# Attention and two gated layers on one core: the short key chunk's products on all 128 rows, and one arrangement of transposed queries with a crossed copy

## The chip, the cores and the metric

The kernel runs on one core of a Trainium2 chip. The metric is the time of one execution on the device in microseconds (us), here the median of three runs. The engines of a core are TensorE (matrix products), VectorE, ScalarE, GpSimd and SyncE, which in this kernel issues the DMA transfers; a profile calls them PE (and PEld for TensorE's weight loads), DVE, ACT, POOL and SP.

## What is computed

There are 4 batches of 8 heads; each head has 576 positions of 64 numbers. Every head is an attention with a learned bias on the scores; the result goes through two feed-forward layers.

```python
scores = scale * np.matmul(q, k.transpose(0, 1, 3, 2))          # 576 x 576 a head
x = (psi_rel / psi_i)[..., None]                                # log distances
bias = np.maximum(x @ w1 + b1, 0.0) @ w2
scores = scores + bias.transpose(2, 0, 1)[None, :, :, :]
scores = scores - np.max(scores, axis=-1, keepdims=True)
attn = np.exp(scores)
attn = attn / (np.sum(attn, axis=-1, keepdims=True) + 1e-09)
y = np.matmul(attn, v)                                          # to 2304 x 512
g = y @ w_gate                                                  # 512 -> 1536
y2 = (g / (1 + np.exp(-g))) * (y @ w_val) @ w_out               # 1536 -> 512
out = np.maximum(y2 @ w_in, 0.0) ** 2 @ w_out2                  # 512 -> 2048 -> 512
```

## The kernel before, in words

**Numbers.** All operands are float32. For the products most of them are split into two float16 parts, a high one (hi) and the residual (lo), and hi·hi, hi·lo and lo·hi are summed, so that one wanted product is two or three products on TensorE.

**Passes.** Attention runs over five query tiles. Four tiles `t` = 0 to 3 hold 128 queries of a head, so each is a pass over 4 × 8 = 32 heads. The fifth, `"m"`, holds the last 64 queries: two heads stand side by side, so it has 16 items. `attend` (L936) takes the items one after the other: `scores` (L801), `soft` (L820, which adds the bias and exponentiates), `soft2` (L842, which transposes the probabilities) and, two items later, `weighted` (L864, the products with the values) and `normalise`. Beside each pass the bias of the next (`make_bias`), the weights and the first feed-forward layer (`moe1`, L459 and L482 its products) are computed; the second layer is worked out behind the attention, from about 770 us on.

**Key chunks.** A head's 576 keys are four chunks of 128 (keys 4·p + r for r = 0 to 3) and a short one of 64. In pass 0 the probabilities stay float32 and are transposed on TensorE; chunk 4 of the transposed probabilities holds the last 128 keys, and only its rows 64 to 127 are multiplied with the values' short chunk (L867). In the other passes a DMA transpose writes `pT` in nine chunks; chunk 4 holds the short chunk's hi part in rows 0 to 63 and its lo part in rows 64 to 127. Per head there are 14 products of 64 or 65 columns; the last, short chunk's hi with the values' lo part, takes rows 0 to 63 alone (`n = 64`, L876). Rows 64 to 127 of that part of the values are zeroed by a memset when they are made (L773). `kv_chunks`, `prep_k` and `turn` (L701, L713, L706) split the keys and transpose them on TensorE, the short chunk as 64 rows.

**Queries.** `prep_q` (L734) prepares four heads' queries of one tile: it loads `qf`, and writes into `qs` per head four blocks of 64 columns: hi, lo, lo, hi (ScalarE L746 both hi, VectorE L747 the residual, VectorE L754 its copy). A transpose makes `qT` of eight blocks of 128 × 128: per head one with hi over lo, and one crossed, lo over hi. `scores` multiplies both with the transposed keys (hi over lo) and sums them. In pass 0 the transposes are TensorE's (`turn`), in the other passes a DMA transpose's (L759). There are 36 such preparations: eight in pass 0, 28 in the other passes. `qs` and `qf` have one buffer each, `qT` has two. `attend` calls `prep_q` for the next four heads when it is at the first head of the present four (in the merged pass at the first item of a batch).

**Order.** The generators are interleaved by costs that stand in the `yield` lines and by a table (`LEAD`), which the change does not touch. The framework then orders each engine's instructions itself, by priorities and a simulated timeline, and puts in all waits on semaphores; on the chip every engine, SyncE among them, runs its list in order. All DMA transfers, the transposes included, are issued by SyncE.

Of the kernel before, what the change touches and what calls it, by code (L numbers as in the profile page):

```python
# [11 lines left out]
F16 = mybir.dt.float16  # L12
# [3 lines left out]
AF = mybir.ActivationFunctionType  # L16
# [8 lines left out]
P = 128  # L25
# [12 lines left out]
SQK = 16.0  # L38
# [37 lines left out]
def tile_attention_moe(  # L76
# [4 lines left out]
    nc = tc.nc  # L81
# [11 lines left out]
    ident_h = res.tile([P, P], F16, name="ident_h")  # L93
# [8 lines left out]
    st = {}  # L102
# [86 lines left out]
    def minus(out_, x, f, hi):  # L189

        nc.vector.scalar_tensor_tensor(
            out=out_, in0=x, scalar=f, in1=hi, op0=ALU.mult, op1=ALU.subtract)
# [21 lines left out]
    def mixed(k):  # L214

        mix_n[k] = mix_n.get(k, -1) + 1
        return MIX[k][mix_n[k] % len(MIX[k])]
# [176 lines left out]
    att = a_stack.enter_context(tc.tile_pool(name="att", bufs=2, side="right"))  # L394
# [5 lines left out]
    def ma():  # L400

        if early[0]:
            return ps_qk.tile([P, 2, 512], F32, tag="qk", name="qk0")[:, 0, :]
        return ps_mm.tile([P, 512], F32, tag="ma", name="ma", bufs=1)
# [248 lines left out]
    def load_kv(h, which):  # L653

        b, g = divmod(h, 2)
        hs = slice(4 * g, 4 * g + 4)
        src, f = ((k, kvroom(h)[0]), (v, kvroom(h)[3]))[which]
        nc.sync.dma_start(
            f[:, 0:1024].rearrange("p (h x) -> p h x", h=4),
            src[b, hs, 0:512, :].rearrange("h (p r) d -> p h (r d)", r=4))  # L660
        nc.sync.dma_start(
            f[64 * which:64 * which + 64, 1024:1280].rearrange("p (h d) -> p h d", h=4),
            src[b, hs, 512:S, :].rearrange("h p d -> p h d"))
# [37 lines left out]
    def kv_chunks(f):  # L701

        x = f.rearrange("p (c d) -> p c d", d=D)
        return [(P, 4, x[:, 0:16]), (64, 1, x[0:64, 16:20])]

    def turn(dst, src, m, n):  # L706

        pt = ma().bitcast(F16)[:, 0:P * m].rearrange("p (h j) -> p h j", h=m)
        for i in range(m):
            nc.tensor.transpose(pt[:, i, 0:n], src[:, i], ident_h[:n, :n])  # L710
        nc.scalar.copy(dst, pt[:, :, 0:n])

    def prep_k(h):  # L713

        b, g = divmod(h, 2)
        kf, ks, kT, _ = kvroom(h)
        for n, m, x in kv_chunks(kf):
            o = ks[:n, 0:4 * m]
            halves(o[:, :, 0, :], o[:, :, 1, :], x, SQK, mixed("K"))
            for i in range(m):  # L720
                r = i if m > 1 else 4
                turn(kT[:, :, P * r:P * r + n], o[:, i::m].rearrange("p h l d -> p h (l d)"), 4, n)
        nc.sync.dma_start(kT_d[b][:, 4 * g:4 * g + 4, :], kT)
        for i in range(2):
            hold["k", b, 2 * g + i] = kT[:, 2 * i:2 * i + 2, :]
        kv_used[0] = h + 1
# [7 lines left out]
    def prep_q(b, t, a):  # L734

        qf = att.tile([P, 4, D], F32, tag="qf", name="qf", bufs=1)
        if t == "m":
            src = q[b, :, 512:S, :].rearrange("(a e) s d -> e s a d", e=2)
            for e in range(2):
                nc.sync.dma_start(qf[64 * e:64 * e + 64], src[e])  # L740
        else:
            nc.sync.dma_start(
                qf, q[b, 4 * a:4 * a + 4, P * t:P * t + P, :].rearrange("h p d -> p h d"))
        qs = att.tile([P, 4, 4, D], F16, tag="qs", name="qs", bufs=1)
        qb = qf.rearrange("p (h o) d -> p h o d", o=1).to_broadcast([P, 4, 2, D])
        nc.scalar.activation(qs[:, :, 0::3, :], qb, AF.Copy, scale=SQK)  # L746
        nc.vector.scalar_tensor_tensor(  # L747
            out=qs[:, :, 1, :], in0=qf, scalar=SQK, in1=qs[:, :, 0, :],
            op0=ALU.mult, op1=ALU.subtract)
        how = mixed("Q")  # L750
        if how:
            nc.scalar.copy(qs[:, :, 2, :], qs[:, :, 1, :])
        else:
            nc.vector.tensor_copy(qs[:, :, 2, :], qs[:, :, 1, :])  # L754
        qT = att.tile([P, 8, P], F16, tag="qT", name="qT")
        if t == 0:
            turn(qT, qs.rearrange("p h (s l) d -> p (h s) (l d)", s=2), 8, P)
        else:
            nc.sync.dma_start_transpose(out=qT, in_=qs.rearrange("p h l d -> p (h l d)"))  # L759
        st["q", b, t, a] = qT  # L760

    cnt = [0]

# [37 lines left out]
    def scores(t, b, n, kts):  # L801

        qT = st["q", b, t, n // 4]
        pq = ps_qk.tile([P, 2, 512], F32, tag="qk", name="qk")
        for j in range(2):
            js = slice(288 * j, 288 * j + 288)
            if t == "m":
                for s in range(2):
                    for e in range(2):
                        nc.tensor.matmul(  # L810
                            pq[64 * e:64 * e + 64, j, 0:288], qT[:, 2 * (n % 4) + s, 64 * e:64 * e + 64],
                            kts[e][:, js], start=s == 0, stop=s == 1)
            else:
                for s in range(2):
                    nc.tensor.matmul(  # L815
                        pq[:, j, 0:288], qT[:, 2 * (n % 4) + s, :], kts[0][:, js],
                        start=s == 0, stop=s == 1)
        return pq

# [22 lines left out]
    def soft2(s, pt, warm=None):  # L842
        pT = att.tile([P, 10, P], F16, tag="pT", name="pT", bufs=3)
        if pt is None:
            pf = pT.rearrange("p a i -> p (a i)").bitcast(F32)
            tr = ps_qk.tile([P, 2, 512], F32, tag="qk", name="tr")
            if warm is not None and av_done[0] < 14:

                for _ in range(2):
                    nc.tensor.matmul(  # L850
                        tr[:, 0, :], ident_h, warm[:, 0:4, :], start=True, stop=True)
            for c in range(4):
                nc.tensor.transpose(tr[:, 0, P * c:P * c + P], s[:, P * c:P * c + P], ident)

            nc.tensor.transpose(tr[:, 1, 0:P], s[:, S - P:S], ident)
            nc.scalar.copy(pf, tr.rearrange("p a j -> p (a j)")[:, 0:640])
            return pf.rearrange("p (c i) -> p c i", i=P)

        rest_of(pt[:, 1, 64:S], s[:, 0:512], pt[:, 0, 0:512])
        rest_of(pt[:, 1, 0:64], s[:, 512:S], pt[:, 0, 512:S])  # L860
        nc.sync.dma_start_transpose(out=pT[:, 0:9, :], in_=pt.rearrange("p l j -> p (l j)"))
        return pT

    def weighted(t, pT, av, slot, vs):  # L864
        if t == 0:
            for c in range(5):
                r = slice(0 if c < 4 else 64, P)  # L867
                nc.tensor.matmul(
                    av[:, slot, 0:64], pT[r, c, :], vs[0][c][r], start=c == 0, stop=c == 4)
            return  # L870
        es = (0, 1) if t == "m" else (0,)
        m = 0
        for c in range(5):

            for l, c0, cn in ((0, 64, 65), (0, 0, 64), (1, 64, 65))[0:3 if c < 4 else 2]:
                n = 64 if c == 4 and c0 == 0 else P  # L876
                for e in es:
                    r = slice(64 * e, 64 * e + 64) if t == "m" else slice(0, P)
                    nc.tensor.matmul(  # L879
                        av[r, slot, 0:cn], pT[:n, 5 * l + c, r], vs[e][c][:n, c0:c0 + cn],  # L880
                        start=m == 0, stop=m == 13)
                m += 1

# [52 lines left out]
    def attend(u0, t, bs, big, feed):  # L936
# [40 lines left out]
        if not first_q[0]:  # L977
            prep_q(bs[0], t, 0)
# [90 lines left out]
    def kvroom(h):  # L1069


        ba = kvb.bitcast(F16)
        if h < 2:
            kT = wr.t.bitcast(F16)[:, 9 + 8 * h:13 + 8 * h, 0:S]
            vr = wr.t[:, 13 + 8 * h:16 + 8 * h, :].rearrange("p a b -> p (a b)")[:, 0:1280]
        else:
            r = kva if h % 2 == 0 else kvb
            kT = r.bitcast(F16)[:, 0:2304].rearrange("p (h s) -> p h s", h=4)
            vr = r[:, 1152:2432]
        ks = ba[:, 4904:4904 + 4 * 512].rearrange("p (c l d) -> p c l d", l=2, d=D)  # L1080
        kf = wof[:, 4864:6144]
        return kf, ks, kT, vr
# [29 lines left out]
                load_kv(n, 1)  # L1112

    def a_stream():
        load_kv(0, 0)
        prep_q(0, 0, 0)
        load_kv(0, 1)
        bias_setup()
        yield from merge((make_bias(0), 25.0), (kv_start(), 6))
        early[0] = False  # L1120
        yield ("go", 0)
        yield from attend(0, 0, (0, 1, 2, 3), x_first, feed_first)
# [211 lines left out]
    def mm2():  # L1334
# [4 lines left out]
        out=g2, in0=st["i2"], scalar1=2.0 / (C1 ** 2 * KR), scalar2=None, op0=ALU.mult)  # L1339
# [148 lines left out]
```

## Time and profile before

| what | value |
|---|---|
| three runs | 1253.57, 1255.06, 1259.63 us; median 1255.06 us |
| the profiled execution | 1258.03 us, its span 1256.0 us |
| busy | PE 1129.9 us (90%), DVE 779.8 (62%), ACT 682.8 (54%), POOL 653.2 (52%) |
| instructions | 27398 |
| mean granted clock of TensorE | 0.963 of full speed |
| DMA | 278078 packets, 163.20 MB; 233276 packets are under 512 B |

The profile holds one execution. Its page gives the busy time of each engine, the span in 40 slices, the DMA queues, the chain of work that ended last (followed back from the last instruction) and groups of instructions by line. Other views answer for a stretch, a line or a tile: instructions in order of time, who waited for whom, busy time by windows. Records of matrix products overlap, since the products are pipelined: what one costs its successors is read from starts, not from its length. A DMA's issue is the time on SyncE; its landing is counted from the start of the issue.

### The profile page before, as it was taken

The page shows a single profiled execution, that of the slowest core. Times are in us where ns is not written, and L with a number is a line of the kernel's source. Part 1 is how long each engine was busy: PE and PEld are TensorE (multiplying, and loading weights), DVE is VectorE, ACT ScalarE, POOL GpSimd, SP SyncE. Part 2 cuts the span into 40 slices and gives each one's busy share as a digit, 9 for nine tenths or more (in the row PEclk, how much of TensorE's full clock was granted, in tenths as well). Part 3 has the DMA queues.
Part 4 walks back from the last instruction along what each step waited for, and adds up shares of the span by engine and source line. Part 5 has one row for each costly group of instructions (what it writes and reads, how often), then busy time and mean ns, then how long its engine had stood idle before and what let it go on. Part 6 is the DMA issues. An engine that isn't in the chain of part 4 may idle for free.

```text
span 1256.0 us, 27398 instructions
## 1 busy us (share of the span) xinstructions
PE 1129.9 (90%) x10550; PEld 833.4 (66%) x10550; DVE 779.8 (62%) x1872; ACT 682.8 (54%) x1386; POOL 653.2 (52%) x837
## 2 busy tenths in 40 slices
PE   2688889999779899999998899979879999999998
PEld 2566778677457668687784676657337577484787
DVE  6998747687668457666674745887474452624423
ACT  4467767547567556656574444367362542615433
POOL 1533213259759569879686463126782441705423
PEclk9998788999969999999999999989999999999999
DMA  8857634128999999998889995670002010010000
GB/s 236 206 158 187 204 107 100 40 68 162 211 219 206 217 207 170 210 218 146 186 177 235 259 214 130 202 225 4 17 2 50 17 35 34 4 47 18 24 28 17
DMA packets 278078, 163.20 MB, mean 130 GB/s; under 512 B 233276, under 2 KB 246588, under 8 KB 277948
## 3 DMA queue, kind: packets, MB, share of 16 engines
q1 hardware_dynamic: 277948, 161.46, 55.5%
q8 instruction: 82, 1.34, 0.4%
q14 instruction: 48, 0.39, 0.1%
HBM read 92.13 MB, written 19.48 MB: 89 GB/s over the span
## 4 chain that ended last, share of the span: by engine, by line
PE 51%; DMA 13%; DVE 9%; POOL 5%; issue 4%; ACT 3%; SPq 1%; POOLq 0%; ACTq 0%; DVEq 0%
PE mm L459 13%; PE mm L1376 12%; PE mm L1408 10%; PE mm L482 4%; DMA pT<-pt 4%; PE av L879 3%; PE qk L815 2%; DMA qT<-qs 2%; POOL x L1188 2%; PE ma L1408 2%; DMA scrap<-in_moe_w_in_dram 2%; DMA w2s<-in_moe_w_out_dram 1%; PE ma L644 1%; POOL pt L220 1%; DMA w2s<-in_moe_w_in_dram 1%
## 5 line engine op out<-in xcount | busy, mean ns | idle before, releaser
L459 PE MATMUL mm<-xT,wr 128*128 128x256 f16 x2400 | 292.3, 278 | 11.6 <-DVE th L470 4.6
L459 PEld LDWEIGHTS <-wr 128*128 128x128 f16 x2592 | 253.4, 100 | 55.9 <-issue 15.7
L1188 POOL TENSOR_TENSOR x<-x 128x256 f32<-128x256 f32 (+1 forms) x160 | 143.0, 905 | 177.9 <-ACT x L1385 171.5
L220 POOL TENSOR_TENSOR pt<-s,pt 128x512 f16<-128x512 f32 x224 | 173.0, 795 | 39.5 <-ACT pt L839 33.7
L220 POOL TENSOR_TENSOR z<-th,z 128x256 f16<-128x256 f32 x108 | 81.0, 751 | 129.3 <-ACT z L444 118.8
L482 PE MATMUL mm<-wr,z 128*128 128x512 f16 x612 | 142.5, 379 | 0.8 <-DVE th L470 0.8
L824 DVE CUSTOM_DVE_ANT_0 s<-qk,room 128x576 f32<-128x576 f32 x144 | 107.7, 749 | 43.1 <-PE qk L815 27.1
L1408 PEld LDWEIGHTS <-wr 128*128 128x128 f16 x1134 | 110.7, 98 | 20.5 <-DVE wr L1188 3.0
L832 ACT ACTIVATE s<-s,sc 128x576 f32<-128x576 f32 x112 | 86.0, 771 | 61.8 <-DVE sc L831 46.5
L1188 DVE TENSOR_TENSOR wr<-x,wr 128x768 f16<-128x768 f32 (+3 forms) x60 | 75.5, 1268 | 64.5 <-ACT wr L1195 63.4
L1376 PE MATMUL mm<-wr,w2r 128*128 128x512 f16 (+1 forms) x480 | 103.2, 366 | 6.5 <-ACT x L1381 6.5
L482 PEld LDWEIGHTS <-z 128*128 128x128 f16 x648 | 59.8, 98 | 66.1 <-issue 1.9
L605 DVE TENSOR_TENSOR scrap<-scrap,room 128x1024 f16<-128x1024 f16 (+1 forms) x108 | 85.6, 807 | 27.5 <-PE ma L644 23.0
L1376 PE MATMUL mm<-wr,room 128*128 128x512 f16 (+1 forms) x480 | 100.1, 358 | 0.0
L879 PE MATMUL av<-vp,pT 128*128 128x65 f16 (+5 forms) x1792 | 82.3, 196 | 19.7 <-DMA pT<-pt 18.3
L879 PEld LDWEIGHTS <-pT 128*128 128x128 f16 (+3 forms) x1792 | 69.3, 101 | 39.0 <-DMA pT<-pt 24.4
L621 POOL TENSOR_TENSOR scrap<-scrap 128x256 f32<-128x256 f32 (+1 forms) x90 | 63.5, 706 | 53.6 <-ACT scrap L620 50.0
L1376 PEld LDWEIGHTS <-w2r 128*128 128x128 f16 x480 | 47.7, 99 | 54.3 <-issue 10.5
L1376 PEld LDWEIGHTS <-room 128*128 128x128 f16 x480 | 47.1, 98 | 45.8 <-issue 0.5
L644 PEld LDWEIGHTS <-scrap 128*128 128x128 f16 x1440 | 60.6, 105 | 24.4 <-DVE scrap L605 10.6
L444 ACT CAST z<-th 128x256 f16<-128x256 f32 x108 | 42.8, 398 | 62.0 <-DVE th L470 60.6
L1427 ACT ACTIVATE ob<-ob,fac 128x256 f32<-128x256 f32 x36 | 17.8, 506 | 105.5 <-DVE ob L1426 105.5
(285 smaller groups left out, 2183.3 us busy)
## 6 DMA issues: line engine op xcount, KB each, us to landing
kp<-kT_d SPq DMA_DIRECT2D x64, 288.0 KB, 3.4
vp<-v_d SPq DMA_DIRECT2D x48, 325.0 KB, 3.7
w2s<-in_moe_w_out_dram SPq DMA_DIRECT2D x16, 512.0 KB, 4.2
wr<-in_moe_w_gate_dram SPq DMA_DIRECT2D x24, 256.0 KB, 5.7
wst<-in_moe_w_out_dram SPq DMA_DIRECT2D x12, 512.0 KB, 4.5
wr<-in_moe_w_val_dram SPq DMA_DIRECT2D x24, 256.0 KB, 4.1
v_d<-vp SPq DMA_DIRECT2D x16, 325.0 KB, 3.4
y_d<-yh SPq DMA_DIRECT2D x18, 256.0 KB, 2.8
```

Of the source, the lines that this page charges most:

```text
L220: nc.gpsimd.tensor_tensor(out=out_, in0=x, in1=hi, op=ALU.subtract)
L459: nc.tensor.matmul(pg[:, 256 * gi:256 * gi + 256], wr.parts(key, f // 4, cc, wl, P * (f % 4), P), mov(xl, cc), start=k == 0, stop=k == 11)
L482: nc.tensor.matmul(po, zall[:, f, zl, P * t:P * t + P], wr.parts("o", 0, f, wl), start=k == 0, stop=k == 3 * NF1 - 1)
L605: nc.vector.tensor_tensor(out=m[:, :, ni * e:ni * e + ni], in0=block(kb, i0, ni), in1=th, op=ALU.is_gt)
L621: nc.gpsimd.tensor_tensor(out=tmp[r], in0=tmp[r], in1=xb, op=ALU.mult)
L644: nc.tensor.matmul(pv[:, :, :, c:c + 4], m[:, a, :], bd[:, l], start=l == 0, stop=l == 1)
L824: nc.vector.tensor_tensor_reduce(out=s.rearrange("p (a j) -> p a j", a=2), in0=pq[:, :, 0:288], in1=bias[:, n].rearrange("p (a j) -> p a j ...
L832: nc.scalar.activation(s, s, AF.Exp, bias=nm, scale=-1.0)
L879: nc.tensor.matmul(av[r, slot, 0:cn], pT[:n, 5 * l + c, r], vs[e][c][:n, c0:c0 + cn], start=m == 0, stop=m == 13)
L1188: (nc.gpsimd if how else nc.vector).tensor_tensor(out=out_, in0=a, in1=b, op=op)
L1376: nc.tensor.matmul(ph[:, :n], w2r.parts("w", g // 4, cc, wl, P * (g % 4), P), yt[:, 4 * yl + cc, :], start=m == 0, stop=m == 11)
L1408: nc.tensor.matmul(po, HS[f][:, o:o + P], st["C7"][f][wl][:, b:b + 256], start=f == 0 and k == 0, stop=f == 7 and k == 2)
```

## The change

The short key chunk's products and transposes take all 128 rows: `kv_chunks` gives the short chunk 128 rows, `turn` transposes with the whole identity matrix, and `weighted` no longer cuts rows. What the added rows hold is zero: five memsets at the start of `a_stream` clear rows 64 to 127 of the keys' room and rows 0 to 63 of four rooms of values, which the loads never write; in the other passes the zeros of L773 serve.

In `prep_q`, for all passes but the first, `qs` has two blocks per head (hi, lo) instead of four, the DMA transpose makes four blocks `qT[:, 0]` instead of eight, and two DMA transfers within SBUF copy its halves crosswise into `qT[:, 1]`. `qT` is now ordered by arrangement first, then by head, in pass 0 also (`pairs`), and `scores` and the warming products of `soft2` take it so.

```diff
-        return [(P, 4, x[:, 0:16]), (64, 1, x[0:64, 16:20])]
+        return [(P, 4, x[:, 0:16]), (64, 1, x[:, 16:20])]
...
-    def turn(dst, src, m, n):
+    def turn(dst, src, m, n, pairs=False):
...
-            nc.tensor.transpose(pt[:, i, 0:n], src[:, i], ident_h[:n, :n])
+            nc.tensor.transpose(pt[:, i % 2 * 4 + i // 2 if pairs else i], src[:, i], ident_h)
...
-            o = ks[:n, 0:4 * m]
+            o = ks[:, 0:4 * m]
...
+        qT = att.tile([P, 2, 4, P], F16, tag="qT", name="qT")
+        st["q", b, t, a] = qT
         qs = att.tile([P, 4, 4, D], F16, tag="qs", name="qs", bufs=1)
+        if t != 0:
+            qs = qs.rearrange("p h l d -> p (h l d)")[:, 0:512].rearrange("p (h l d) -> p h l d", h=4, l=2)
+            nc.scalar.activation(qs[:, :, 0, :], qf, AF.Copy, scale=SQK)
+            minus(qs[:, :, 1, :], qf, SQK, qs[:, :, 0, :])
+            nc.sync.dma_start_transpose(out=qT[:, 0], in_=qs.rearrange("p h l d -> p (h l d)"))
+            for e in range(2):
+                nc.sync.dma_start(qT[64 * e:64 * e + 64, 1], qT[64 - 64 * e:128 - 64 * e, 0])
+            return
...
-                        pq[:, j, 0:288], qT[:, 2 * (n % 4) + s, :], kts[0][:, js],
+                        pq[:, j, 0:288], qT[:, s, n % 4, :], kts[0][:, js],
...
-                r = slice(0 if c < 4 else 64, P)
                 nc.tensor.matmul(
-                    av[:, slot, 0:64], pT[r, c, :], vs[0][c][r], start=c == 0, stop=c == 4)
+                    av[:, slot, 0:64], pT[:, c, :], vs[0][c], start=c == 0, stop=c == 4)
...
-                n = 64 if c == 4 and c0 == 0 else P
...
-                        av[r, slot, 0:cn], pT[:n, 5 * l + c, r], vs[e][c][:n, c0:c0 + cn],
+                        av[r, slot, 0:cn], pT[:, 5 * l + c, r], vs[e][c][:, c0:c0 + cn],
...
     def a_stream():
+        nc.gpsimd.memset(kvroom(0)[0][64:P, 1024:1280], 0.0)
+        for h in range(4):
+            nc.gpsimd.memset(kvroom(h)[3][0:64, 1024:1280], 0.0)
```

## Rows read from the trace of the kernel before

**Rows 1.** Busy time by windows: window, length, then each engine, clock, DMA share, GB/s.
```profile
66.00:220.00 154.00, 135.98 (x1021) 111.47 (x1021) 117.20 (x296) 107.66 (x227) 40.16 (x44) 0.87 0.55 148
287.00:400.00 113.00, 93.47 (x1071) 69.94 (x1069) 81.94 (x213) 75.00 (x166) 89.79 (x125) 0.88 0.97 207
400.00:700.00 300.00, 282.44 (x3230) 215.41 (x3228) 189.65 (x571) 175.91 (x377) 223.77 (x334) 0.99 0.96 199
```

**Rows 2.** The chain of work that ended last, shares of the span by line.
```profile
PE mm L459 13%; PE mm L1376 12%; PE mm L1408 10%; PE mm L482 4%; DMA pT<-pt 4%; PE av L879 3%; PE qk L815 2%; DMA qT<-qs 2%; POOL x L1188 2%; PE ma L1408 2%; DMA scrap<-in_moe_w_in_dram 2%; DMA w2s<-in_moe_w_out_dram 1%; PE ma L644 1%; POOL pt L220 1%; DMA w2s<-in_moe_w_in_dram 1%
```

**Rows 3.** Groups by form (rows*columns): count, busy us, mean ns, idle before.
```profile
L879 PE MATMUL av<-vp,pT 64*128 64x64 f16 x96 | 19.3, 201 | 0.0
```

**Rows 4.** TensorE's timeline, one head's products: start us, us, what, count; three narrow windows.
```profile
401.41 0.69 PE L879 MATMUL av<-vp,pT 128*128 128x65 f16 x14
...
401.77 0.32 PE L879 MATMUL av<-vp,pT 128*128 128x65 f16 x2
...
401.89 0.20 PE L879 MATMUL av<-vp,pT 64*128 64x64 f16 x1
402.03 0.28 PE L459 MATMUL mm<-xT,wr 128*128 128x256 f16 x1
```

**Rows 5.** TensorE's timeline, one head of pass 0; the middle row from a narrow window.
```profile
113.92 1.36 PE L868 MATMUL av<-kva,pT 128*128 128x64 f32 x10
...
114.65 0.53 PE L868 MATMUL av<-kva,pT 128*128 128x64 f32 x2
...
115.22 0.29 PE L710 MATMUL ma<-ident_h,room 128*128 128x128 f16 x2
```

**Rows 6.** Tile qs: ns min/median/max; the last: idle us and times until.
```profile
L746 ACT ACTIVATE qs<-qf x36: 612/630/641, 6.0 to 709.2; 128x512 f16<-128x512 f32 x36
L754 DVE COPY qs<-qs x36: 205/226/1176, 8.0 to 710.3; 128x256 f16<-128x256 f16 x36
...
  DMA qT<-qs: 25.2, 14
```

**Rows 7.** Lines 444 and 773: a 256-column conversion, a memset.
```profile
L444 ACT CAST z<-th x108: 386/404/429, 177.1 to 878.4; 128x256 f16<-128x256 f32 x108
...
L773 POOL MEMSET vp<- x16: 201/201/232, 217.8 to 407.9; 64x128 f16 x16
```

**Rows 8.** Tile qT: the transposes' issue in ns, and landing.
```profile
L759 SPq DMA_TRANSPOSE qT<-qs x28: 1231/1267/2683, 200.9 to 722.0; - x28
...
DMA to landing us min/median/max: 3.0/3.9/5.8
```

**Rows 9.** Tile xT, 740 to 800 us: four transposes of four blocks each.
```profile
L929 SPq DMA_TRANSPOSE xT<-xh x4: 1190/1223/1257, 774.9 to 778.8; - x4
...
DMA to landing us min/median/max: 2.4/2.5/3.0
```

**Rows 10.** Tile junk, 287 to 500 us: loads of 64 partitions, issue and landing.
```profile
L778 SPq DMA_DIRECT2D junk<-in_v_dram x26: 595/622/1240, 304.8 to 408.1; - x26
...
DMA to landing us min/median/max: 2.4/3.3/4.5
```

**Rows 11.** SyncE's timeline around one transpose of queries.
```profile
350.34 1.27 SPq L759 DMA_TRANSPOSE qT<-qs  x1
351.71 2.96 SPq L861 DMA_TRANSPOSE pT<-pt  x2
355.12 0.34 SPq L799 DMA_DIRECT2D v_d<-vp  x1
```

**Rows 12.** SyncE's waits: us in total, times, longest.
```profile
SPq L861 <- POOL room L627: 28.6, 15, 4.1
...
SPq L283 <- DMA wst<-in_moe_w_out_dram: 7.1, 3, 4.7
```

**Rows 13.** TensorE's idle time until `pT` landed (tile pT); its waits for `qT`, 287 to 500 us.
```profile
  DMA pT<-pt: 42.7, 39
...
PE qk L815 <- DMA qT<-qs: 4.1, 2, 3.5
```

More of the change, by code (lines that the diff above doesn't have):

```diff
@@ L754, in prep_q @@
             nc.vector.tensor_copy(qs[:, :, 2, :], qs[:, :, 1, :])
[L755 to L760, printed above, removed]
+        turn(qT.rearrange("p s h i -> p (s h) i"), qs.rearrange("p h (s l) d -> p (h s) (l d)", s=2), 8, P, True)
     cnt = [0]
@@ L810, in scores @@
                         nc.tensor.matmul(
-                            pq[64 * e:64 * e + 64, j, 0:288], qT[:, 2 * (n % 4) + s, 64 * e:64 * e + 64],
+                            pq[64 * e:64 * e + 64, j, 0:288], qT[:, s, n % 4, 64 * e:64 * e + 64],
                             kts[e][:, js], start=s == 0, stop=s == 1)
@@ L850, in soft2 @@
                     nc.tensor.matmul(
-                        tr[:, 0, :], ident_h, warm[:, 0:4, :], start=True, stop=True)
+                        tr[:, 0, :], ident_h, warm[:, 0], start=True, stop=True)
             for c in range(4):
```

## The prediction, made before the changed kernel was run

> **What bounds the kernel now.** I read the windows by stage first [rows 1]. TensorE has a record running for 94% of 400–700 us, for 88% of 66–220 us and for 83% of 287–400 us. GpSimd comes next (75 and 79% in the two later windows), and the DMA engines stand at 0.96 and 0.97 there. So from 400 us on TensorE sets the pace; before that it is one of several. The page's chain of waits agrees: TensorE's lines lead it, and the DMA transposes of probabilities and queries hold 4 and 2% [rows 2].
>
> Then the forms of TensorE's products. Almost all use the whole array; the short key chunk's products use 64 of 128 rows: 96 of them in the three float16 passes of 128 queries [rows 3], and a pair for each of the merged pass's 16 heads. A record's length hides what they cost, since records overlap; starts show it. One head's 14 products begin at 401.41 us, the 13th starts at 401.77, the 14th, the half-row one, at 401.89, and the next whole-row product of another tile at 402.03 [rows 4]. Twelve whole-row steps thus take 0.36 us, 0.03 each; the step into the half-row product takes 0.12 and the step out 0.13–0.14. TensorE empties itself on each change of arrangement. The idle time before these products is nil, so no view of waits shows this.
>
> **What the change does, part by part** (against the profiled execution: span 1256.0 us, 1258.0 us with what lies around it; the three timed runs' median, 1255.06, is 3 us lower, and I carry the difference over to it).
>
> *Full rows, 128-query passes.* A head's 0.62 us becomes 14 × 0.03 = 0.42: 0.20 us × 96 heads = 19.2 us of TensorE.
>
> *Merged pass.* Its heads lie in 64 columns, so leaving for other work changes the arrangement anyway; only the switch into the half-row pair goes, about 0.10 us (0.12 against about 0.03 [rows 4]) × 16 = 1.6 us.
>
> *First pass, float32.* Ten records take 1.30 us (113.92 to 115.22), while the first seven steps take 0.73, 0.104 each [rows 5]; ten whole-row steps at 0.104 to 0.11 would be 1.07 us. 0.23 × 32 heads = 7.4 us.
>
> *Key transposes.* Eight groups of four half-row transposes lose two switches of 0.1 us, and their moving side doubles; I take 1 us off, bounded by 0 and 1.6.
>
> In all TensorE loses 29 us of occupation. How much of this reaches the end is my choice, by window. In 400–700 us, three quarters of what 64 heads save (12.8) is 9.6; merged pass 1.2; at 287–400 us, where TensorE waits more often, a third of 6.4, or 2.1; in the first pass, 0.4 of 8.4, or 3.4. Sum 16.3; bounds 0 and 29.
>
> A rule speaks against filling the rows. Rows 4 show whole-row products 0.03 us apart although each has a weight load of its own. The Trainium skill (TensorE: Matmul & The Clock Gate, Part 3: Packing small matmuls) says a weight load overlaps running matmuls only when their row groups differ; by that, whole-row products could never follow so closely, and the half-row ones would be the cheap ones. The trace contradicts it here; by the rule the saving would vanish and the sum would be the queue's cost alone, near 1261.
>
> *Queries, computing.* In 28 of 36 preparations ScalarE writes 256 instead of 512 columns. That is 630 ns before [rows 6]; the nearest 256-column conversion is 0.40 us [rows 7]. VectorE's copy (226 ns) goes. That is 6 us on each, both only half busy. ScalarE also stands 25.2 us in 14 waits for a transpose to release `qs` [rows 6]. The transpose now carries four blocks instead of eight: with eight it lands in 3.0 to 5.8 us [rows 8], and the last unit's four-block ones in 2.4 to 3.0 us, in a quiet stretch [rows 9]. So each such wait shrinks by some 0.6 us, 8 us in all. Hidden by work on TensorE and GpSimd; I take 1.5 us of gain, bounds 0 and 8.
>
> *Queries, the queue.* The issue does not shrink with the blocks: 1.22 us with four [rows 9], 1.27 with eight [rows 8]. Added are 56 copies of 64 partitions, whose nearest row, a 64-partition load, takes 0.62 us to issue and 2.4 to 4.5 us to land [rows 10]. They sit on SP, which also issues every transpose of probabilities, and SP is dense at times: from 350.34 to 355.12 us three issues take 4.2 of 4.8 us [rows 11]. The first copy cannot go before the transpose has landed; whatever stands behind it on SP (probabilities, keys, values) waits too. If it is queued directly behind the transpose, SP stands 2.6 us (landing 3.9 less issue 1.27); if other issues lie between, not at all. I take 0.8. So 28 × (2 × 0.62 + 0.8) = 57 us of SP's time; bounds 35 and 107. Much of it falls into time in which SP waits anyway: the longest of its waits for GpSimd before a transpose of probabilities adds up to 28.6 us [rows 12]. I let a quarter of the 57 delay a transpose, and a third of that reach TensorE (39 waits on probabilities for 112 transposes [rows 13]): 5 us. Bounds 0 and 25.
>
> *Queries, later arrival.* The crossed half is there 0.62 + 3.3 us [rows 10] after the transpose, less the 0.6 that it gains: about 3.3 us later. The attention loop asks for them four heads ahead, and TensorE waits for a query tile just twice, 4.1 us together [rows 13]. Both waits would grow by 3; with a few near misses I take 3 us, bounds 0 and 10.
>
> *Memsets.* Five at the start on GpSimd, each some 0.4 us by the nearest row (201 ns for half the columns [rows 7]), before the loads that they stand beside have landed: nothing, at most 2 us.
>
> **Sum:** −16.3 − 1.5 + 5 + 3 = −9.8, about −10: 1248 for the profiled execution, 1245 for the median.
>
> **Rivals.**
> *All of the emptying is returned.* For it: 94% of 400–700 us is TensorE's. Against: waits on probabilities, 42.7 us over both its sides. With 0.9 of 29 returned and the copies hidden: 1255 − 26 = 1229.
> *It turns slower: SP stands at the landing.* Its place is SP between transpose and first copy, above all in 287–415 us, where eight preparations would add 8 × (1.24 + 2.6) = 31 us to a queue that is nearly full in the stretch shown [rows 11]. Priced at the high bounds, 25 for SP, less 16 of TensorE's gain: 1264. It decides once SP stands over about 2.5 us in most of the 28, with no ready issue placed between. For it: SP has stood on a DMA's landing before, 4.7 us at the longest [rows 12]. Against: the order on SP interleaves the issues of different heads [rows 11], so others may stand between. The Trainium skill (DMA: Bandwidth & Descriptors, Rules for kernel authors) asks for this very wait before a DMA that reads what another wrote; the trace of before has no such pair back to back.
> *The gain turns into waiting.* TensorE frees itself, GpSimd's residuals and the DMA transposes do not come sooner; only the first pass and a few us of the rest come back, and the queue takes them: 1254. For it: GpSimd at 79% in 287–400 us and the DMA engines near 0.97 [rows 1]. Against: little idle time at 94%.
>
> **Chances.** My sum, as 1236 to 1249: 0.48. All returned: 0.17. Gain into waiting: 0.20. Slower by SP: 0.15. A measurement of this kernel can tell 0.5% (6 us) from no change. Faster by more than that: 0.46 of the first case and the second, 0.63; within: 0.02 and the third, 0.22; slower 0.15. The range runs from the second case to short of the fourth, 1229 to 1262.
>
> **What would show it.** Right: no 64-row products in the forms; a head's 14 products 0.42 us from first to the next tile; TensorE's instruction count about unchanged with its occupation near 1105 us; waits on `qT` a few us longer. SP's part: pauses between `qT`'s transpose and its first copy, well under 1 us on average. Wrong: pauses of 2 us and more with longer waits on probabilities (the slower rival); or TensorE's idle time grown by as much as its records shrank (the third).

## The result and the profile after

The changed kernel took 1269.24 us (median of six runs, 1265.09 to 1270.49), the kernel before 1255.95 us beside it. The ratio is 1.0109 with a 95% interval of 1.0085 to 1.0133: slower by 1.1%, where 1245 us had been forecast. The profiled execution took 1265.09 us with a span of 1263.2 us.

The part of the page that answers to the table of before, the engines' busy time:

```profile
span 1263.2 us, 27437 instructions
...
PE 1100.3 (87%) x10550; PEld 814.1 (64%) x10550; DVE 778.8 (62%) x1844; ACT 676.4 (54%) x1386; POOL 650.0 (51%) x842
```

TensorE's records cover 29.6 us less than the 1129.9 of before, for the same 10550 products, and the span is 7.2 us longer. All other engines have about as much to do. So TensorE does less and waits more: its idle time grew by 36.8 us, from 126.1 to 162.9. The forms of the products with the values and one head on TensorE's timeline (answering to [rows 3, 4]):

```profile
L882 PE MATMUL av<-vp,pT 128*128 128x65 f16 x864 | 56.3, 197 | 42.0 <-DMA pT<-pt 34.0 <-DVE x L902 3.5 <-issue 2.5
L882 PE MATMUL av<-vp,pT 128*128 128x64 f16 x480 | 55.6, 196 | 0.0
L882 PE MATMUL av<-vp,pT 128*64 128x65 f16 x288 | 10.9, 200 | 2.2 <-DMA pT<-pt 1.8 <-DMA vp<-v_d 0.3
L882 PE MATMUL av<-vp,pT 128*64 128x64 f16 x160 | 10.2, 197 | 0.0
```

```profile
486.65 0.59 PE L882 MATMUL av<-vp,pT 128*128 128x65 f16 x14
487.08 0.49 PE L459 MATMUL mm<-xT,wr 128*128 128x256 f16 x3
```

No half-row form is left, and the 14 products of one head take 0.43 us to the next tile's first (486.65 to 487.08), as reckoned. But the idle time before the first of them has risen: 34.0 us of it ended with a transpose of probabilities, against 17.0 for the same form before. For the whole tile `pT` (answering to [rows 13]):

```profile
  DMA pT<-pt: 80.8, 80
```

It was 42.7 us in 39. But this sum takes both of TensorE's sides, the weight loads and the products, which stand at the same time almost throughout; so it counts most of the waiting twice. The products alone, in the view of waits, first before, then after:

```profile
PE av L879 <- DMA pT<-pt: 18.3, 16, 3.2
```

```profile
PE av L882 <- DMA pT<-pt: 35.8, 38, 3.4
```

That is 17.5 us more, about half of what TensorE's idle time grew by. The next largest part is the wait of the score products for the keys (`kp`), which rose from 3.0 to 10.4 us. Keys, like the probabilities, come by transfers that SyncE issues.

Where in the execution the time is lost is read from the first and the last start of the later passes' products with the values (tile `pT`, first before, then after):

```profile
L879 PE MATMUL av<-vp,pT x1792: 190/193/246, 292.3 to 767.9; 128*128 128x65 f16 x97, 128*128 128x64 f16 x42, 128*64 128x65 f16 x31, 128*64 128x64 f16 x16
```

```profile
L882 PE MATMUL av<-vp,pT x1792: 190/193/263, 284.6 to 774.7; 128*128 128x65 f16 x97, 128*128 128x64 f16 x53, 128*64 128x65 f16 x33, 128*64 128x64 f16 x17
```

The part ahead of them became 7.7 us shorter, the passes after the first 14.5 us longer (475.6 to 490.1), and the rest stayed (488.1 and 488.5). Counted by starts, the first two of these passes (tiles 1 and 2) take 263.5 us before and 275.1 after, so most of the loss is there.

What SyncE does for the queries, in the view of tile `qT` (answering to [rows 8]; the landing is now over transposes and copies together), and its waits (us in total, times, longest):

```profile
L753 SPq DMA_DIRECT2D qT<-qT x56: 467/558/632, 195.9 to 741.3; - x56
...
L751 SPq DMA_TRANSPOSE qT<-qs x28: 1188/1248/2499, 192.0 to 733.9; - x28
...
DMA to landing us min/median/max: 1.9/2.6/5.9
```

```profile
SPq L866 <- POOL room L627: 27.8, 19, 3.4
...
SPq L753 <- DMA qT<-qs: 18.7, 17, 2.8
```

56 copies take 0.56 us each to issue, 31 us, and SyncE stands 18.7 us for the transposes' landing. One of the long cases on SyncE's timeline: after the transpose at 557.88 and one load it stands from 559.79 to 562.57, and the transpose of probabilities behind the copies starts at 564.42.

```profile
557.88 1.28 SPq L751 DMA_TRANSPOSE qT<-qs  x1
559.21 0.58 SPq L772 DMA_DIRECT2D kp<-kT_d  x1
562.57 1.11 SPq L753 DMA_DIRECT2D qT<-qT  x2
...
564.42 1.50 SPq L866 DMA_TRANSPOSE pT<-pt  x1
```

GpSimd's last residual for that transpose ended at 561.76, so SyncE's other work held this one up by some 2.7 us. In the sum no such delay was added. From the end of GpSimd's last residual to the start of the issue, the 112 transposes of probabilities take 138.1 us in all before and 138.7 after, and SyncE's waits ahead of them add up to 131.5 us in 94 cases before and 123.2 in 90 after.

### The profile page after: what moved, and what is told of

It reads as the page before. It is cut to its first block, busy times and chain, and to the rows that moved or that the text cites. A ratio compares the mean times of both kernels' runs of the same rounds, so it can differ in the third digit from the quotient of the medians.

```text
span 1263.2 us, 27437 instructions
## 1 busy us (share of the span) xinstructions
PE 1100.3 (87%) x10550; PEld 814.1 (64%) x10550; DVE 778.8 (62%) x1844; ACT 676.4 (54%) x1386; POOL 650.0 (51%) x842
## 4 chain that ended last, share of the span: by engine, by line
PE 44%; DMA 18%; DVE 14%; POOL 10%; issue 7%; ACT 5%; SPq 2%; POOLq 0%; ACTq 0%; DVEq 0%
PE mm L1382 12%; PE mm L1414 10%; PE mm L459 10%; DMA pT<-pt 5%; POOL pt L220 3%; PE mm L482 3%; DMA wr<-in_moe_w_gate_dram 2%; DMA qT<-qs 2%; POOL x L1194 2%; PE ma L1414 2%; PE av L882 2%; DMA w2s<-in_moe_w_out_dram 2%; DVE scrap L605 1%; PE qk L820 1%; DVE wr L265 1%
## 5 line engine op out<-in xcount | busy, mean ns | idle before, releaser
L220 POOL TENSOR_TENSOR z<-th,z 128x256 f16<-128x256 f32 x108 | 78.2, 725 | 118.0 <-ACT z L444 109.6
L882 PE MATMUL av<-vp,pT 128*128 128x65 f16 (+3 forms) x1792 | 70.7, 197 | 44.2 <-DMA pT<-pt 35.8
L605 DVE TENSOR_TENSOR scrap<-scrap,room 128x1024 f16<-128x1024 f16 (+1 forms) x108 | 89.2, 841 | 29.5 <-PE ma L644 23.6
L882 PEld LDWEIGHTS <-pT 128*128 128x128 f16 (+1 forms) x1792 | 61.2, 103 | 61.2 <-DMA pT<-pt 45.0
L644 PEld LDWEIGHTS <-scrap 128*128 128x128 f16 x1440 | 60.9, 105 | 25.8 <-DVE scrap L605 12.0
L820 PE MATMUL qk<-kp,qT 128*128 128x288 f16 x384 | 67.5, 299 | 8.0 <-DMA kp<-kT_d 7.3
```

The costliest lines, as they stand in the source:

```text
L220: nc.gpsimd.tensor_tensor(out=out_, in0=x, in1=hi, op=ALU.subtract)
L605: nc.vector.tensor_tensor(out=m[:, :, ni * e:ni * e + ni], in0=block(kb, i0, ni), in1=th, op=ALU.is_gt)
L820: nc.tensor.matmul(pq[:, j, 0:288], qT[:, s, n % 4, :], kts[0][:, js], start=s == 0, stop=s == 1)
L882: nc.tensor.matmul(av[r, slot, 0:cn], pT[:, 5 * l + c, r], vs[e][c][:, c0:c0 + cn], start=m == 0, stop=m == 13)
```

## The experiments

Every ratio below is to the kernel before, timed beside the experiment on the same chip. The theory after the result, A: SyncE's extra work (issues and waits) makes the probabilities' transposes late. (The last count above speaks against this path; the runs below show what the copies cost.) Its rivals: B, the framework's new order of instructions fits the chip less well; and late arrival of the crossed halves.

### The two parts apart

`e1_rows_only` is the kernel before with the row part of the change alone; `e2_queries_only` is the changed kernel with the row part undone.

```diff
 # e1: of the change, only
+        return [(P, 4, x[:, 0:16]), (64, 1, x[:, 16:20])]
...
+            nc.tensor.transpose(pt[:, i], src[:, i], ident_h)
...
+                    av[:, slot, 0:64], pT[:, c, :], vs[0][c], start=c == 0, stop=c == 4)
...
+                        av[r, slot, 0:cn], pT[:, 5 * l + c, r], vs[e][c][:, c0:c0 + cn],
+        # and the five memsets
 # e2: the same lines as before the change, the rest as changed
```

> The full rows, the whole identity and the memsets alone; queries as before (eight-block transpose, no copies). Theory A (SyncE: 56 copies and the waits for the transposes' landing hold up the transposes of probabilities; the rows themselves gain): 1232 to 1242, TensorE busy near 1100 us, idle time until pT lands near before's 42.7 us. Theory B (any change reshuffles the framework's order of instructions, and the new order fits the chip less well; the freed TensorE time turns into waiting): 1250 to 1262, idle time until pT lands 60 us and more.

> The queries' four-block transpose with two copies within SBUF alone; short chunk on 64 rows as before. Theory A: the copies' cost undiluted, 1272 to 1290, since nothing is gained against it; idle time until pT lands 70 us and more. Theory B: 1255 to 1268, no special tie to the copies; rows and queries each worth little by themselves.

The rows alone: 1249.35 us, ratio 0.9948 (0.9923 to 0.9973). The queries alone: 1273.28 us, 1.0140 (1.0091 to 1.0189). So the queries cost 1.4% and the rows give 0.5%: A in its direction. In e2, however, the idle time until `pT` lands is only 56.5 us (both sides), where A had asked for 70 and more; the kernel with the copies waits less for the probabilities there than e1, which is faster. And the rows give less than A had said (1232 to 1242), and their idle time until `pT` lands, in the profile of e1, is

```profile
  DMA pT<-pt: 73.6, 67
```

and not near 42.7. Part of TensorE's saving became waiting although no copy was there.

### What of the queries costs: engine, time of issue, wait

`e3_dve_copies` lets VectorE make the crossed halves, `e4_copies_later` asks for the copies two heads later.

```diff
 # e3
-                nc.sync.dma_start(qT[64 * e:64 * e + 64, 1], qT[64 - 64 * e:128 - 64 * e, 0])
+                nc.vector.tensor_copy(qT[64 * e:64 * e + 64, 1], qT[64 - 64 * e:128 - 64 * e, 0])
 # e4: prep_q appends qT to a list; in attend, ahead of the scores
+            if idx == 0 or n % 4 == 2:
+                cross()
```

> The changed kernel with the crossed halves copied by VectorE (two 64-partition copies of 512 columns, some 0.3 us each) instead of two DMA transfers: SyncE has 56 issues and 28 waits fewer, the arrival of the crossed half is earlier, and VectorE gets 56 instructions and may stand for the landing. Theory A: 1232 to 1246, idle time until pT lands falls back to 40 to 55 us. Theory B: 1255 to 1272, as the changed kernel within the spread of orders. If late crossed halves were the cause, it gains too, but TensorE's waits for qT would have to fall by more than 10 us, of which the changed kernel's trace shows none.

> The changed kernel with the two copies asked for two heads after their transpose instead of at once: the same 56 issues, no wait for the landing (18.7 us of recorded waits, 21 us counted, go). Theory A with the wait as the main cost: 1245 to 1256; Theory A with the issues and their place among the probabilities' transposes as the main cost: 1260 to 1270, SyncE's waits for qT gone and the time little moved. Theory B: anywhere in 1255 to 1272.

e3: 1259.98 us, 1.0031 (1.0006 to 1.0057), some 10 us better than the changed kernel and 10 worse than the rows alone; that is in B's range and outside A's (1232 to 1246). In its waits VectorE now stands where SyncE stood:

```profile
DVE qT L753 <- DMA qT<-qs: 35.3, 20, 4.8
```

The wait was moved, not removed, so e3 speaks for A only in part. Against late arrival speaks the changed kernel's own trace: TensorE waits 1.1 us there for `qT`. e4: 1275.44 us, 1.0169 (1.0123 to 1.0216). It failed as a test: the framework put the copies close behind their transposes again, and SyncE's wait for `qT` is still there, 19.1 us in 16 cases.

### Copies left out, and copies that wait for nothing

`e5_no_cross` leaves the crossed copies out; `scores` multiplies the uncrossed arrangement twice, so the cross terms are missing from the scores. `e6_free_copies` adds to it 56 copies of the same size that read `qs` and go nowhere useful. `e9_tiny_copies` moves 32 bytes a partition in each of the 56, `e10_one_copy` makes 28 copies of 128 partitions of them. In all four the products' number and shape stay. The last column is the length of the passes after the first in the profiled execution, read as above; it is 475.6 us before.

```diff
 # e5
-                nc.sync.dma_start(qT[64 * e:64 * e + 64, 1], qT[64 - 64 * e:128 - 64 * e, 0])
...
-                        pq[:, j, 0:288], qT[:, s, n % 4, :], kts[0][:, js],
+                        pq[:, j, 0:288], qT[:, 0, n % 4, :], kts[0][:, js],
...                       # the same in the merged pass
 # e6, on top of e5 (for e in range(2))
+                    qs_all[64 * e:64 * e + 64, 512:1024], qs_all[64 - 64 * e:128 - 64 * e, 0:512])
 # e9 in its place
+                    qs_all[64 * e:64 * e + 64, 512:528], qs_all[64 - 64 * e:128 - 64 * e, 0:16])
 # e10 in its place, once
+            nc.sync.dma_start(qs_all[:, 512:1024], qs_all[:, 0:512])
```

> The changed kernel without the crossed copies: scores multiply the uncrossed arrangement twice (the cross terms of the two halves are left out, the products' number and shape stay). If the copies (their 56 issues, their waits for the landing) are the queries' cost: 1238 to 1250, as the rows alone or better. If something else in the queries' edit costs it (an order that fits less well, the qT buffer taken earlier), it stays at 1256 to 1270.

> As the one without crossed copies, but with 56 copies of the same size issued right behind the transposes that read qs instead of qT and are read by nobody: the issues and the traffic are there, the wait for the transpose's landing is not. If the issues on SyncE are the cost: 1260 to 1270, as the changed kernel. If the wait for the landing is (21 us counted): 1245 to 1255. In between, 5 us and more on either side, both.

> As the 56 free copies (no crossed halves, scores use the uncrossed arrangement twice), but each copy moves 32 bytes a partition instead of 1024: the issues stay, the traffic is a thirty-second. If SyncE's issue time is the cost: 1260 to 1270, as with the full copies. If the traffic on the DMA engines is: 1246 to 1254, as without copies.

> As the 56 free copies, but one copy of 128 partitions in place of two of 64: 28 issues, the same bytes in all. If the number of issues is the cost: about half of the 18 us, 1255 to 1262. If the traffic is: 1262 to 1270.

| kernel | copies on SyncE | us | ratio (95%) | passes, us |
|---|---|---|---|---|
| e5 | none | 1249.40 | 0.9962 (0.9939 to 0.9985) | 475.8 |
| e10 | 28, all bytes | 1254.90 | 0.9996 (0.9974 to 1.0017) | 480.2 |
| e9 | 56, 1/32 of the bytes | 1263.95 | 1.0067 (1.0048 to 1.0087) | 488.1 |
| e6 | 56, all bytes, no wait for the landing | 1267.14 | 1.0098 (1.0062 to 1.0134) | 493.4 |
| changed kernel | 56, all bytes, with that wait | 1269.24 | 1.0109 (1.0085 to 1.0133) | 490.1 |

Without copies the kernel stands where the rows alone stand: nothing else in the queries' edit costs anything that can be told. By ratios of 1255 us, 28 issues cost 4 us, 56 tiny ones 13, 56 full ones 17; the wait for the landing adds 1.4, inside the intervals. So the copies are the cost, and their number weighs more than their bytes: 0.15 to 0.30 us of kernel time for each. Finer steps than that are not shown, since the intervals of e9 and e6 overlap and the framework's order differs in each of these kernels. The copies of e6, e9 and e10 also hold `qs` longer, but ScalarE's waits for its release are no longer for that (30.6 us in e5, 32.2 in e6, 21.7 in e9, 29.5 in e10). Nor does the path through late transposes show here: the products' waits for `pT` are 31.1 us in e5, 37.2 in e10, 33.3 in e9 and 35.8 in e6. The issues were of about equal length throughout; tiny and full ones in the view of tile `qs`, first e9, then e6:

```profile
L754 SPq DMA_DIRECT2D qs<-qs x56: 467/534/628, 191.9 to 736.3; - x56
```

```profile
L754 SPq DMA_DIRECT2D qs<-qs x56: 461/587/1117, 194.2 to 730.5; - x56
```

### ScalarE's wait for qs, and an order alone

`e7_two_halves` uses the two halves of one `qs` tile in turn; `e8_other_mix` is the kernel before with one number of the interleaving changed.

```diff
 # e7, with qs_room a tile made once
...
+            half[0] = 512 - half[0]
+            qs = qs.rearrange("p h l d -> p (h l d)")[:, half[0]:half[0] + 512].rearrange("p (h l d) -> p h l d", h=4, l=2)
 # e8
-            gens = [(attend(2 + 2 * i, t, (0, 1, 2, 3), big, feed_of(t)), 55.0)]
+            gens = [(attend(2 + 2 * i, t, (0, 1, 2, 3), big, feed_of(t)), 56.5)]
```

> The changed kernel with qs as one tile whose two halves are taken in turn, so that ScalarE no longer waits for the previous transpose to release it (33.9 us in 12 waits in the changed kernel). If ScalarE's standing there is what makes the probabilities late: 1245 to 1258. If it is hidden or SyncE alone sets them: 1262 to 1272, with those waits gone.

> The kernel before with the attention's weight in the interleaving at 56.5 instead of 55: the same instructions in another order. It measures what an order alone is worth. If the framework's reshuffling explains the changed kernel: a move of 10 us and more either way. If an order alone is worth little: 1250 to 1260.

e7: 1266.70 us, 1.0087 (1.0061 to 1.0113), the changed kernel within the intervals. It is inconclusive on its own question, because the wait did not go: in its profile ScalarE stands for the transposes of `qs` 29.0 us in 11 cases, in the changed kernel 33.9 in 12.

e8: 1261.07 us, 1.0053 (1.0029 to 1.0077). The same instructions in another order cost 7 us. B is real at that size. It does not make the series above by itself: six kernels have 56 copies on SyncE, each in an order of its own (changed, e2, e4, e6, e7, e9), and all are 0.7 to 1.7% slower than the kernel before, while none without them is more than 0.53% slower (e8). But no single difference of a few us between reshuffled kernels can be put down to its edit alone.

### The rows with the order held

In `e12_rows_late` one line differs from the kernel before, and the instructions and their order on all engines are those of before.

```diff
-                n = 64 if c == 4 and c0 == 0 else P
+                n = P
```

> The kernel before with one line changed: the half-row products of the passes after the first take all 128 rows (112 heads' items; the zeros that this needs are there already). The instructions and their order on every engine are exactly those of before, so no reshuffling is in it. If TensorE's emptying sets the pace there: 20.8 us of it go and 12 to 18 come back, 1237 to 1243. If these passes wait for the probabilities' transposes anyway: the time TensorE saves turns up as idle time before the products with the values, 1251 to 1256.

1254.11 us, 0.9991 (0.9965 to 1.0018): 1 us, with some 3 either way. In its profile the passes after the first take 473.9 us, against 475.6. TensorE's records cover 24.9 us less than before, and the idle time until `pT` lands is 65.6 us on both sides, 28.8 on the products' side (18.3 before):

```profile
PE 1105.0 (88%) x10550; PEld 815.5 (65%) x10550; DVE 777.6 (62%) x1872; ACT 681.3 (54%) x1386; POOL 654.9 (52%) x837
```

```profile
  DMA pT<-pt: 65.6, 57
```

```profile
PE av L879 <- DMA pT<-pt: 28.8, 27, 3.1
```

This is the cleanest result here: in the passes after the first, what TensorE no longer spent on emptying came back as idle time, 20.2 us of it (from 126.1 to 146.3). About half is the products' wait for the probabilities (10.5 us); the rest is spread over many small waits.

The rows' 0.5% then belongs to the first pass and the keys. The profiles bear this out: in the 13 kernels that have the whole rows there, the later passes' first product with the values starts at 282.9 to 287.8 us (285.8 in the mean), in the four that have not (before, e2, e8, e12) at 289.3 to 292.3 (291.3). That is 5.5 us.

### What sets the pace of those passes

`e11_qf_on_act` issues 32 loads of queries on ScalarE's queue. `e13_fewer_issues` loads the values' short chunk once a pair instead of twice and lets ScalarE write it to both halves of the partitions. `e14_hi_on_act` makes all high halves of the probabilities on ScalarE, and `e15_both` is e13 and e14 together. All stand on the rows alone (e1).

```diff
 # e11
+            (nc.scalar if t else nc.sync).dma_start(
...                       # in the merged pass nc.scalar too
 # e13
-            for i in range(2):
...
-                    raw[1][64 * i:64 * i + 64].rearrange("p (h d) -> p h d", h=2),
+                raw[1][0:64].rearrange("p (h d) -> p h d", h=2),
...
-        nc.scalar.activation(o[:, :, 64:128], x, AF.Copy, scale=sv)
+        for e in range(2):
+            nc.scalar.activation(o[64 * e:64 * e + 64, :, 64:128], x[0:64], AF.Copy, scale=sv[64 * e:64 * e + 64])
 # e14
-    "V": (0,), "b": (2, 0), "B": (2,), "h": (0,), "H": (0, 1), "x": (0, 0, 1),
+    "V": (0,), "b": (2, 0), "B": (2,), "h": (0,), "H": (0,), "x": (0, 0, 1),
```

> The rows alone, with the 32 loads of queries of the passes after the first issued by ScalarE's queue instead of SyncE's. If SyncE's issues set the pace of these passes (56 issues cost 18 us, 0.3 us each), taking 32 off gives about 10 us back: 1236 to 1244 against 1249. If it is not SyncE's room but what comes behind (order, GpSimd), or if ScalarE pays for it: 1246 to 1258.

> The rows alone, with 16 issues fewer on SyncE in the passes' first: the values' short chunk is loaded once a pair into rows 0 to 63 instead of twice, and ScalarE writes its high part to both halves of the partitions (16 small instructions more). If SyncE's issues set the pace there at the copies' 0.25 to 0.3 us each: 1244 to 1246 against 1249, and faster than anything so far. If SyncE has room without the copies: 1248 to 1252.

> The rows alone, with the high halves of all probabilities made by ScalarE: GpSimd loses 56 conversions of 0.67 us (38 us), ScalarE gains as many. If GpSimd sets when the probabilities' transposes can go: 1235 to 1245. If it does not, or ScalarE becomes the late one: 1249 to 1265.

> The rows alone with both: 16 issues fewer on SyncE, and all high halves of the probabilities made by ScalarE. If the two act on different delays: 6 and 8 us add up, 1233 to 1238 where the rows alone stand at 1249. If they act on one and the same, or ScalarE becomes the late one: 1240 to 1246.

| kernel | us | ratio (95%) |
|---|---|---|
| e1, rows alone | 1249.35 | 0.9948 (0.9923 to 0.9973) |
| e11 | 1257.57 | 1.0025 (0.9998 to 1.0051) |
| e13 | 1243.13 | 0.9894 (0.9875 to 0.9912) |
| e14 | 1241.21 | 0.9880 (0.9846 to 0.9914) |
| e15 | 1234.54 | 0.9844 (0.9817 to 0.9872) |

e11 missed: it is 8 to 10 us slower than the rows alone although SyncE issues 32 loads less, and why is not shown. e13 gained 6 to 7 us for 16 issues, e14 8 to 9 us, and together 13: they nearly add up. In e15's profile ScalarE has 39 us more to do than in e1 (720.2), GpSimd 41 less (614.3), and the idle time until `pT` lands is down from 73.6 to 60.9 us on both sides:

```profile
  DMA pT<-pt: 60.9, 53
```

In e14 it is not down (73.0), though the kernel is faster. The time from GpSimd's last residual to the transposes' issue, 134 us in all in e1, is 112 in e13, 85 in e14 and 78 in e15. This fits the reading that GpSimd's residuals and SyncE's issues each set a part of the pace of these passes; it does not prove it, since the order was held in none of them. e15, with the queries as they were, beats both kernels by 1.6 and 2.6%.

## Why the prediction was wrong

The forecast was 10 us faster, the kernel came out 13 us slower. Two steps of the sum make most of the 24 us between 1245 and 1269: the worth of TensorE's emptying in the later passes (some 12 us) and the worth of SyncE's time (some 13).

- **TensorE's emptying: right in size, wrong in worth.** The 29 us were there (29.6 less in the records). The step that failed is the choice of how much reaches the end: 12.9 us were put on the passes after the first ("three quarters", "a third", the merged pass's 1.2); e12, with the order held, gave 1 us. A busy share of 94% was read as TensorE setting the pace. Part of that share was the emptying itself, and without it TensorE stood idle instead, for the next `pT` in about half of that time. The third rival ("the gain turns into waiting") describes this part.
- **The first pass and the keys: 3.4 us forecast,** some 5.5 by the profiles: right in kind, a little low.
- **The queue's time: right.** 57 us of SyncE's time were reckoned. In the trace it is 31 us of issues, and counted over all 28 transposes SyncE stands 21 us before the first copy, 0.75 each against the 0.8 taken.
- **The queue's worth: the second failed step.** "A quarter of the 57 delays a transpose, a third of that reaches TensorE" made 5 us. It cost 18 (1.0109 less 0.9962 of e5, times 1255). The path was wrong too, as far as the traces tell: in the sum the transposes of probabilities do not go out later behind their data (138.7 us against 138.1), and SyncE waits ahead of them nearly as much as before (in the largest group 27.8 us against 28.6). Yet the copies cost their 18 us. TensorE's added waits are spread over probabilities and keys; by which path the copies cause them stays open.
- **A count read too high.** The "39 waits on probabilities for 112 transposes" are 16 of products and 23 of weight loads, mostly for the same transposes; in the changed kernel 38 and 42.
- **The slower rival** had the right sign, 1264 us, and about the right place (its 287 to 415 us lie in the two passes that lost most). But its mechanism, SyncE standing at the landing, is worth 1.4 us by the runs, inside the intervals; it was to decide at 2.5 us of standing in most groups, and the mean was 0.75, with 3 of 28 over 2.5. In 27 of 28 other issues stood between the transpose and its first copy.
- **Later arrival: 3 us forecast.** In the changed kernel's trace the score products and their weight loads wait 1.1 us in two cases for `qT`, where it was 9.1 in five; nothing was lost there.
- **ScalarE's waits** were to shrink by 8 us. They grew from 25.2 to 33.9. They are 30.7 in e1, which has no copies and transposes of eight blocks, so the copies are not the main reason; it stays open.
- **The rule on weight loads** (the Trainium skill, TensorE: Matmul & The Clock Gate, Part 3: Packing small matmuls) is contradicted in the changed kernel too: 14 whole-row products, each with a weight load of its own, and the step to the next tile take 0.43 us, 0.03 each.

What stays open besides the copies' path: how much of each late experiment's gain is its order. e8 shows that an order alone can be worth 7 us, and only e12 held it.

## What to carry to other kernels

A drain or a stall on an engine is worth its length only where nothing else is late at the same place; before counting it, look at what the next instruction would have waited for. A queue that waits often need not have room: when its transfers are what the other engines wait for, an added transfer can cost a good part of its issue (here a quarter to a half of the 0.56 us). So try to save issues (one transfer instead of two) before saving work on a busier-looking engine: here 24.9 us less in TensorE's records gave 1 us, and 16 issues less gave 6 to 7, though with another order. Don't add up the waits of weight loads and of products, which stand together. Compare with the order of instructions held where it can be, because a planner's reshuffling alone may move the time by as much as the edit.

## What the runs showed of the hardware that had not been expected

- A copy of 32 bytes a partition on 64 partitions takes about as long to issue (534 ns in e9) as one of 1024 bytes (587 ns in e6), and one of 128 partitions about as long as one of 64 (534 ns in e10): for these copies the issue does not go by bytes.
- A DMA transpose of four blocks takes about as long to issue as one of eight (1248 against 1267 ns), though it lands a little earlier (median 3.3 us in e5, where no copies are mixed in, against 3.9 before and 3.6 in e1).
- A change of the array's rows between products costs about 0.1 us each way on TensorE ([rows 4]: steps of 0.12 to 0.14 us instead of 0.03), in time that the records count as busy.
